# Second layers of a mixture of experts taken half by half, with longer runs of half-width output blocks, and logits transposed in the middle of the value products

## The chip, the cores and the metric

One core of a Trainium2 chip runs the whole kernel. The metric is the device time of one execution in microseconds (us), as the median of several executions. Lower is better.

## The reference

Causal attention with a per-step decay (8 batches, 8 heads, 576 positions, head size 64) is followed by a soft mixture of 8 experts. Cut to what matters here:

```python
scores = q @ k.T / 8 + cum[i] - cum[j]          # causal
x = softmax(scores) @ v                          # reshaped to 4608 rows x 512
logits = x @ phi                                 # 4608 x 32: 8 experts x 4 slots
d = softmax(logits, axis=0)                      # over the rows
slot_input = d.T @ x                             # 32 x 512
for e in range(8):                               # w1: 512 x 1024, w2: 1024 x 512
    slot_out[e] = relu(slot_input[e] @ w1[e]) @ w2[e]
c = softmax(logits, axis=1)                      # over the 32 slots
out = c @ slot_out                               # 4608 x 512, float32
```

All inputs and outputs are float32. The expert weights are 33.6 MB, the output is 9.4 MB.

## The kernel before, in words

**Attention.** The loop runs over 32 pairs of heads (`g`, four pairs to a batch). The order of all instructions is written out by hand, so each engine works through its queue in program order. For a pair, `s1` and `tops` find row maxima of the scores (TensorE, then VectorE), `s2` and `expo` make the exponentials (TensorE, then ScalarE), `causal` blanks the upper triangle (GpSimd), and `s3` multiplies them with the values: 50 small products in the order of the list `VALUES`, with 64 output partitions each, written to `pv`. `norm` divides by the row sums and writes `X`; `px` and `xcopy` transpose `X` for the logits.

**Logits of a batch.** One batch behind the attention, its logits are worked on amid the pairs; `w` counts the pairs from 0 to 3. At `w == 0` `logits` multiplies with phi. The result is 32 slots by 576 positions, folded into 128 partitions: columns 0 to 127 of the tile `LG` hold four blocks of 128 positions, and columns 128 to 191 of partitions 0 to 31 hold the last 64 positions. At `w == 1` `weigh` copies them to `LG`, `mgroup`, `mtop` and `mcast` find and spread the running maximum, `weigh2` makes the exponentials `EX`, `total` keeps the running sum `lrun`, and `tokens` transposes both `EX` and `LG` into one PSUM tile (`tk`), from which `LD` (the dispatch weights) is copied by ScalarE, and which `combine(b, 0)` reads on VectorE. `tk` takes its turn among three PSUM tiles (`ps_s`, tag `s`) with the score tiles of `s1`. The last 64 positions must come out in two partition halves, so they are doubled before the transpose: GpSimd copies them to the spare columns 192 to 255 of `EX`, and a second 128-wide transpose turns columns 128 to 255.

**Experts.** The weights come in quarters of 512 KB (`quarter`, 27 resident tiles and then buffers that have come free), all issued on SyncE's queue (`wload`, `wstream`) in the order that `STEPS` gives. `(e, 0)` is the first layer of expert e (four quarters, `mlp1`), `(e, 4)` and `(e, 6)` are two quarters each of its second layer (`mlp2`). For the experts below `DEFER` = 4 the quarters are cut by rows of w2 and give all 512 output columns at once; for the others (e, 4) gives columns 0 to 255 (half 0) and (e, 6) columns 256 to 511 (half 1). The results add up in PSUM in tiles of 32 partitions x 4.

**Output.** When half 0 of all experts is complete, `gathered`, `slots` and `halve` add up the four partition groups and spread the slot outputs to `SO`, in two float32r parts. `blocks` then multiplies the combine weights (`cT`, transposed by `cols`, two or three transposes at a step of `next(c[b])`) with `SO`, 128 rows of the output at a time; ScalarE and VectorE copy the results to a staging buffer in turn, and SyncE's queue sends it. Blocks with 256 columns (`half[0]`, `half[1]`) write 1 KB pieces to each output row, blocks with all 512 columns 2 KB pieces. The program before interleaves them with the half 1 products of experts 4 to 7 only:

```python
    mlp2(6, 1)
    blocks(2, 4, half[0])
    blocks(4, 6, half[0])
    mlp2(7, 1, 0)
```

13 of the 36 blocks go out in two halves, 23 whole.

Of the kernel before, what the change touches and what calls it, by code (L numbers as in the profile page):

```python
# [31 lines left out]
DEFER = 4  # L32

STEPS = tuple((e, 0) for e in range(8)) + tuple((e, k) for e in range(DEFER) for k in (4, 6)) + tuple((e, k) for k in (4, 6) for e in range(DEFER, 8))

SPLITS = {(6, 0): 4, (0, 6): 2, (1, 6): 3, (2, 6): 5, (3, 4): 6, (4, 4): 7}
# [39 lines left out]
def attn_softmoe(ctx: ExitStack, tc: tile.TileContext, qk, v, f, phi, w1, w2, cst, out):  # L76
# [314 lines left out]
    def weigh(b):  # L391
        if batch(b):
            plg = st["lg", b]
            if b < B - 1:
                nc.scalar.copy(LG[:, 0:128], plg[:, 0:128])
                nc.scalar.copy(LG[0:32, 128:192], plg[0:32, 128:192])
                nc.gpsimd.tensor_copy(EX[96:128, 192:256], LG[0:32, 128:192])  # L397
            else:
                nc.scalar.copy(LG[:, 0:192], plg[:, 0:192])
                nc.gpsimd.tensor_copy(EX[96:128, 192:256], LG[0:32, 128:192])  # L400
# [25 lines left out]
    def weigh2(b):  # L426
# [3 lines left out]
        if b < B - 1:  # L430
            nc.scalar.activation(EX[:, 0:192], LG[:, 0:192], AF.Exp, bias=mb[:, 1:2], accum_out=mb[:, 2:3])
            nc.gpsimd.tensor_copy(EX[0:32, 192:256], EX[0:32, 128:192])
        else:
            nc.scalar.activation(EX[:, 0:192], st["lg", b][:, 0:192], AF.Exp, bias=mb[:, 1:2])
            nc.vector.tensor_copy(EX[0:32, 192:256], EX[0:32, 128:192])
# [3 lines left out]
    def total(b):  # L439
# [5 lines left out]
        elif b < B - 1:  # L445
            nc.scalar.activation(lrun, lrun, AF.Identity, scale=mb[:, 3:4], bias=mb[:, 2:3])
# [3 lines left out]
    def tokens(b, *ns):  # L450
# [91 lines left out]
    nc.gpsimd.memset(EX[:, 192:256], 0.0)  # L542
# [182 lines left out]
    for g in range(1, NG):  # L725
# [19 lines left out]
        if w == 2:  # L745
            combine(b, 0)
# [98 lines left out]
        round_k(g + 3)  # L845
        if w == 1:
            weigh2(b)
            total(b)
        round_q(g + 3)
# [4 lines left out]
        if g == 31:  # L854
# [3 lines left out]
            split(1, 0)  # L858
        s3(g, VALUES[30:])
        if w == 0:  # L860
            logits(b, *range(NPAIR))
        if w == 1:
            tokens(b, 0, 1)
# [31 lines left out]
    next(c[0])  # L895
    tokens(b, 1)
    split(1, 1)
# [66 lines left out]
    def mlp2(e, half, *ks):  # L964

        for k in ks or range(2):
            w = weights(e, 4 + 2 * half + k)
            for n in range(4 if e >= DEFER else 2):
                if e < DEFER:
                    fc, to = 4 * half + 2 * k + n, pv[0]  # L970
                    start, stop = e == half == 0, e == DEFER - 1 and half == 1
                else:
                    fc, to = 4 * k + n, po[half][:, 0:256]
                    start, stop = e == DEFER and k == 0, e == NE - 1 and k == 1
                m = to.shape[1]
                step = m if start or stop else 256
                for c in range(0, m, step):
                    nc.tensor.matmul(  # L978
                        to[32 * (fc % 4) : 32 * (fc % 4) + 32, c : c + step],
                        HT[e][:, fc // 2, fc % 2, :],  # L980
                        w[:, m * n + c : m * n + c + step],
                        start=start,
                        stop=stop,
                    )
# [7 lines left out]
    for e, k in STEPS[:-4]:  # L992
# [26 lines left out]
        if (e, k) == (0, 6):  # L1019
# [4 lines left out]
        if (e, k) == (3, 6):  # L1024
            nc.scalar.copy(so, pv[0])
# [4 lines left out]
    stage = [t.rearrange("p a b -> p (a b)") for t in RAW] + p2 + p0  # L1030
    copies = [nc.scalar.copy, nc.vector.tensor_copy]

    def gathered(n):

        nc.vector.tensor_tensor(so[:, half[n]], so[:, half[n]], po[n][:, 0:256], op=ALU.add)
# [30 lines left out]
    mlp2(4, 1)  # L1066
    slots(0)
    mlp2(5, 1)
    halve(0)
    ring += [po[0], bank[0]]  # L1070
    blocks(0, 2, half[0])
    mlp2(6, 1)
    blocks(2, 4, half[0])
    blocks(4, 6, half[0])
    mlp2(7, 1, 0)
    blocks(6, 8, half[0])
# [61 lines left out]
```

## Time and profile before

| | |
|---|---|
| median of 3 runs | 390.42 us (388.98 to 390.79) |
| the profiled execution | 389.33 us, of which 387.6 us from its first to its last instruction |
| TensorE (PE) busy | 368.5 us, 95% of the span |
| VectorE (DVE), ScalarE (ACT), GpSimd (POOL) busy | 279.2, 274.3, 254.8 us |
| share of PE in the chain of work that ended last | 89% (DMA 3%, ACT 2%, DVE 2%) |
| DMA | 93.72 MB, mean 242 GB/s |

The chain of work that ended last is followed back from the last instruction to what released each step. PE stands for 89% of it. PEld is TensorE's weight load, SPq SyncE's queue. Matmuls are pipelined: the next one can start before the one ahead of it has ended, so a step between two starts says more than a duration. A float32 matmul leaves two records in the trace, a transpose or a float32r matmul one.

### The profile page before, as it was taken

How to read it: one execution, taken by the hardware profiler on the slowest of the kernel's cores; microseconds unless marked ns; L12 is line 12 of the kernel's file. 1: busy time of each engine (PE TensorE's matmuls, PEld its weight loads, DVE VectorE, ACT ScalarE, POOL GpSimd, SP SyncE). 2: the span in 40 equal slices, each digit the busy share in tenths (PEclk: the TensorE clock that was granted, in tenths of full speed). 3: DMA queues.
4: the chain of work that ended last, by engine and by line, in shares of the span. 5: the costliest groups of instructions: out<-in, count | busy, mean ns of one | idle time of the engine just before them, and what ended most of it. 6: DMA issues, size and time to landing. Idle time of an engine off the chain costs nothing.

```text
span 387.6 us, 15148 instructions
## 1 busy us (share of the span) xinstructions
PE 368.5 (95%) x5863; PEld 330.8 (85%) x5863; DVE 279.2 (72%) x1079; ACT 274.3 (71%) x670; POOL 254.8 (66%) x357
## 2 busy tenths in 40 slices
PE   8999999999999999999999999999999998999870
PEld 8889999999999999999999999999999985567640
DVE  7878787878887888788878887888787535441671
ACT  8969887878787878787878787878787553021560
POOL 4987887878787878787878787878787821000000
PEclk9999999999999999999999999999999999999995
DMA  6785878777777777777777777777777989996798
GB/s 206 199 203 153 241 223 269 201 226 201 231 210 218 214 214 215 215 216 213 214 215 217 212 215 215 215 216 214 212 224 208 280 316 361 416 418 258 269 391 317
DMA packets 34344, 93.72 MB, mean 242 GB/s; under 512 B 4266, under 2 KB 8288, under 8 KB 34272
## 3 DMA queue, kind: packets, MB, share of 16 engines
q1 hardware_dynamic: 34272, 92.75, 76.8%
q8 instruction: 46, 0.75, 0.8%
q14 instruction: 26, 0.21, 0.2%
HBM read 63.93 MB, written 9.73 MB: 190 GB/s over the span
## 4 chain that ended last, share of the span: by engine, by line
PE 89%; DMA 3%; ACT 2%; DVE 2%; issue 1%; POOL 1%; SPq 0%; ACTq 0%; POOLq 0%; DVEq 0%
PE pv L315 23%; PE ring L283 14%; PE s L230 13%; PE ring L284 12%; PE pv L342 4%; PE pv L978 4%; PE more L938 4%; PE lg L389 3%; PE ring L511 2%; PE ds L475 2%; DMA out<-RAW 2%; PE ring L1055 1%; DMA YA<-mr 1%; ACT PTS L290 1%; DMA WA<-cumd 1%
## 5 line engine op out<-in xcount | busy, mean ns | idle before, releaser
L290 ACT ACTIVATE PTS<-ring 128x320 f32<-128x320 f32 (+2 forms) x256 | 119.1, 501 | 39.1 <-PE ring L284 31.8
L283 PE MATMUL ring<-YA,WA 67*128 67x320 f32 (+9 forms) x384 | 119.0, 323 | 0.1
L246 DVE CUSTOM_DVE_ANT_0 s<-s,mask 128x320 f32<-128x320 f32 (+3 forms) x256 | 109.6, 446 | 5.6 <-PE s L230 0.9
L284 PE MATMUL ring<-YB,WB 128*128 128x320 f32 (+4 forms) x384 | 110.4, 296 | 0.0
L315 PE MATMUL pv<-V,PTS 128*64 128x65 f32 x3200 | 102.3, 223 | 0.1
L315 PEld LDWEIGHTS pv<-V,PTS 128*64 128x64 f32 x3200 | 97.2, 138 | 3.1 <-issue 1.6
L230 PE MATMUL s<-WA,YA 66*128 66x288 f32 (+9 forms) x384 | 97.9, 310 | 1.0 <-ACT YA L188 0.4
L209 POOL TENSOR_TENSOR WB<-RAW,WB 64x576 fp32r<-64x576 f32 x64 | 90.4, 1413 | 10.9 <-ACT WA L570 4.6
L214 POOL TENSOR_TENSOR YB<-RAW,YA 64x576 fp32r<-64x576 f32 x64 | 89.7, 1419 | 2.6 <-POOL EX L397 0.2
L283 PEld LDWEIGHTS ring<-YA,WA 67*128 67x128 f32 (+3 forms) x384 | 69.0, 181 | 5.8 <-issue 2.1
L284 PEld LDWEIGHTS ring<-YB,WB 128*128 128x128 f32 (+1 forms) x384 | 70.0, 182 | 0.0
L230 PEld LDWEIGHTS s<-WA,YA 66*128 66x128 f32 (+1 forms) x384 | 62.9, 190 | 6.8 <-ACT PTS L290 1.7
L301 POOL TENSOR_SCALAR_AFFINE_SELECT PTS<-PTS 128x128 f32<-128x128 f32 (+1 forms) x128 | 31.5, 268 | 21.9 <-ACT PTS L290 20.3
L246 DVE DVE_READ_ACCUMULATOR2_ANT MT<- 128x1 fp32r x310 | 44.0, 142 | 0.0
L183 ACT CAST WA<-RAW 64x576 fp32r<-64x576 f32 x64 | 40.2, 669 | 3.0 <-DMA RAW<-in_qk 2.1
L298 POOL TENSOR_SCALAR_AFFINE_SELECT PTS<-PTS 128x384 f32<-128x384 f32 x64 | 33.4, 523 | 12.2 <-ACT PTS L290 8.3
L188 ACT CAST YA<-RAW 64x576 fp32r<-64x576 f32 x64 | 40.3, 670 | 0.4
L246 DVE CUSTOM_DVE_ANT_0 s<-s,mask,MT 128x288 f32<-128x288 f32 x62 | 32.6, 526 | 10.0 <-PE s L230 1.4
L342 PE MATMUL pv<-cs,X 128*128 128x128 f32 x155 | 36.5, 272 | 0.0
L330 DVE TENSOR_SCALAR rl<-pv 128x5 f32<-128x5 f32 x64 | 10.5, 164 | 35.0 <-PE pv L315 24.7
L335 DVE TENSOR_TENSOR X<-pv,rl 128x320 f32<-128x320 f32 (+1 forms) x65 | 31.5, 486 | 2.4 <-DMA YA<-mr 0.3
L244 DVE TENSOR_REDUCE MT<-s 128x1 fp32r<-128x288 f32 x62 | 27.9, 450 | 0.0
(220 smaller groups left out, 386.5 us busy)
## 6 DMA issues: line engine op xcount, KB each, us to landing
w<-in_w SPq DMA_DIRECT2D x45, 512.0 KB
RAW<-in_qk SPq DMA_DIRECT2D x31, 576.0 KB
V<-in_v SPq DMA_DIRECT2D x32, 325.0 KB
YB<-YA SPq DMA_DIRECT2D x30, 288.0 KB
WB<-WA SPq DMA_DIRECT2D x30, 288.0 KB
p<-in_w SPq DMA_DIRECT2D x6, 512.0 KB
out<-RAW SPq DMA_DIRECT2D x6, 512.0 KB
out<-p SPq DMA_DIRECT2D x5, 512.0 KB
```

The costliest lines, as they stand in the source:

```text
L183: nc.scalar.copy(WA[g % 3][0:64, S * h : S * h + S], RAW[g % 3][64:128, h])
L188: nc.scalar.copy(YA[g % 3][0:64, h, 64:640], RAW[g % 3][0:64, h])
L209: nc.gpsimd.tensor_tensor(t[0:64], RAW[g % 3][64:128, h], t[64:128].bitcast(F32), op=ALU.subtract)
L214: nc.gpsimd.tensor_tensor(YB[g % 2][64:128, h], RAW[g % 3][0:64, h], YA[g % 3][0:64, h, 64:640].bitcast(F32), op=ALU.subtract)
L230: nc.tensor.matmul(t[:, o : o + w], ya[0:m, h, 128 * blk : 128 * blk + 128], wa[0:m, j0 : j0 + w], start=True, stop=True)
L246: nc.vector.tensor_tensor_reduce(out=t[:, o : o + w], in0=t[:, o : o + w], in1=mask[:, m0 : m0 + w], scale=1.0, scalar=top.bitcast(F32) if ...
L283: nc.tensor.matmul(o, wa[0:m, j0 : j0 + n], ya[0:m, h, 64 + i0 : 64 + i0 + w], start=True, stop=False)
L284: nc.tensor.matmul(o, wb[:, j0 : j0 + n], yb[:, h, i0 : i0 + w], start=False, stop=True)
L290: nc.scalar.activation(PT[i % 2][:, SEG_O[bank] : SEG_O[bank] + at], t[:, 0:at], AF.Exp, scale=0.125)
L298: nc.gpsimd.affine_select(d3, d3, pattern=[[0, 3], [1, 128]], compare_op=ALU.is_ge, fill=0.0, base=0, channel_multiplier=-1)
L315: nc.tensor.matmul(pvv[h][64 * u : 64 * u + 64, t, :], PT[h][:, at : at + 64], V[:, g % 2, c, 65 * h : 65 * h + 65], start=(c == 0), stop= ...
L342: nc.tensor.transpose(pm[:, 0:128], x[:, t, 128 * (p % 2) : 128 * (p % 2) + 128], ident)
```

## The change

It does five things.

- `STEPS` takes the second layers as half 0 of all eight experts, then half 1 of all. `DEFER` is gone, w2 is laid out by column halves for every expert, and both halves add up in one [128, 256] tile each.
- Blocks leave in half width in 12 runs of `early` (27 of 36 blocks, in groups of at most six between the half 1 products of experts 2 to 7); 9 blocks are left whole. Four more staging buffers are used. `cols` steps are spread differently.
- `tokens` transposes columns 0 to 127 as before, but turns the last 64 positions by two matmuls with a 32 x 32 identity, one for each partition half. The doubling copies of `EX` and `LG` go.
- At `w == 1` `tokens` and `combine(b, 0)` stand between the first 30 and the last 20 products of `s3`, instead of behind `s3` and in the next pair. Half of the rounding copies of ScalarE move behind them. The running sum moves from ScalarE to GpSimd.
- In the last batch `split(1, 1)` stands ahead of `tokens(b, 1)`.

```diff
-DEFER = 4
-STEPS = tuple((e, 0) for e in range(8)) + tuple((e, k) for e in range(DEFER) for k in (4, 6)) + ...
+STEPS = tuple((e, k) for k in (0, 4, 6) for e in range(8))
...
-            nc.gpsimd.tensor_copy(EX[0:32, 192:256], EX[0:32, 128:192])
...
-            nc.scalar.activation(lrun, lrun, AF.Identity, scale=mb[:, 3:4], bias=mb[:, 2:3])
+            nc.gpsimd.tensor_scalar(lrun, lrun, mb[:, 3:4], mb[:, 2:3], op0=ALU.mult, op1=ALU.add)
...
-        if 1 in ns:
-            nc.tensor.transpose(pm[:, 0:128], EX[:, 0:128], ident)
-        nc.tensor.transpose(pm[:, 128:256], EX[:, 128:256], ident)
-        if 0 in ns:
-            nc.tensor.transpose(pm[:, 256:384], LG[:, 0:128], ident)
+        for n in sorted(ns):
+            x, o = (LG, 256) if n == 0 else (EX, 0)
+            nc.tensor.transpose(pm[:, o : o + 128], x[:, 0:128], ident)
+            for u in range(2):
+                nc.tensor.matmul(pm[64 * u : 64 * u + 64, 224 - 96 * n : 256 - 96 * n], x[0:32, 128:192], ident[0:32, 0:32], start=True, stop=True)
...
+        if w == 1:
+            tokens(b, 0, 1)
+            combine(b, 0)
+            round_k(g + 3, 1)
+            round_q(g + 3)
         s3(g, VALUES[30:])
...
-        if w == 1:
-            tokens(b, 0, 1)
...
+    split(1, 1)
     tokens(b, 1)
-    split(1, 1)
...
     gathered(0)
-    mlp2(4, 1)
+    mlp2(0, 1)
     slots(0)
-    mlp2(5, 1)
     halve(0)
+    mlp2(1, 1)
+    more(5)
     ring += [po[0], bank[0]]
...
+    early = (((0, 2), (2, 4), (4, 6)), ((6, 8), (18, 20), (20, 22)), ((22, 24), (24, 27)), ((8, 10), (10, 12)), (), ((12, 15),), ((15, 18),))
+    turns = (5, 2, 2, 3, 3)
+    for e in range(2, NE):
+        for n in early[e - 2]:
+            blocks(*n, half[0])
+        mlp2(e, 1)
+        if e < NE - 1:
+            more(turns[e - 2])
     gathered(1)
...
+    for k, n in enumerate(n for run in early for n in run):
+        blocks(*n, half[1])
+        if k in (5, 8):
+            more(7)
+    for n in range(27, NT, 2):
+        blocks(n, min(n + 2, NT))
```

What this moves on TensorE at `w == 1`, before (`tk` is the tile of `tokens`, L315 the value products, L283 and L284 the next pair's scores):

```order
L315 MATMUL pv_150<-V,PTS 64x65 x21
L456 MATMUL tk_2643<-cs,EX 128x128
L457 MATMUL tk_2643<-cs,EX 128x128
L459 MATMUL tk_2643<-cs,LG 128x128
L283 MATMUL ring_152<-YA_93,WA_94 128x448
L284 MATMUL ring_152<-YB_91,WB_92 128x448
```

And in the changed program (line numbers are lower by one to five there):

```order
L314 MATMUL pv_150<-V,PTS 64x65
L452 MATMUL tk_2619<-cs,LG 128x128
L454 MATMUL tk_2619<-cs,LG 64x32 x2
L452 MATMUL tk_2619<-cs,EX 128x128
L454 MATMUL tk_2619<-cs,EX 64x32 x2
L314 MATMUL pv_150<-V,PTS 64x65 x20
L282 MATMUL ring_152<-YA_93,WA_94 128x448
L283 MATMUL ring_152<-YB_91,WB_92 128x448
```

Three transposes behind the values became two transposes and four matmuls of 64 output partitions ahead of the last 20 value products.

On TensorE at the end, before, from half 0 of the last expert on (L978 a quarter of a second layer, four matmuls; L1038 is `slots`, L1055 a block):

```order
L978 MATMUL pv_150<-w_121,w_136 32x256 x4
L978 MATMUL pv_149<-w_122,w_133 32x256 x4
L978 MATMUL pv_149<-w_123,w_133 32x256 x4
L1038 MATMUL more_5700<-ctok,cs 128x256
L978 MATMUL pv_149<-w_124,w_134 32x256 x4
L978 MATMUL pv_149<-w_125,w_134 32x256 x4
L1055 MATMUL ring_153<-SO,cT 128x256
L1055 MATMUL ring_151<-SO,cT 128x256
L978 MATMUL pv_149<-w_126,w_135 32x256 x4
L978 MATMUL pv_149<-w_127,w_135 32x256 x4
```

And in the changed program, from the same place (L966 a quarter, L1024 `slots`, L1041 a block, L705 the transposes of `cols`):

```order
L966 MATMUL pv_150<-w_113,w_136 32x256 x4
L966 MATMUL pv_149<-w_114,X_99 32x256 x4
L966 MATMUL pv_149<-w_115,X_99 32x256 x4
L1024 MATMUL more_5706<-ctok,cs 128x256
L966 MATMUL pv_149<-w_116,X_100 32x256 x4
L966 MATMUL pv_149<-w_117,X_100 32x256 x4
L705 MATMUL ring_153<-cs,w_136 128x128 x2
L1041 MATMUL ring_151<-SO,cT 128x256
L1041 MATMUL lg_5625<-SO,cT 128x256
L1041 MATMUL ring_152<-SO,cT 128x256
L1041 MATMUL ring_153<-SO,cT 128x256
L1041 MATMUL pv_150<-SO,cT 128x256
```

The first block stands eight quarters earlier in the work of the second layers; behind `slots` 14 quarters of half 1 are left instead of 6.

On VectorE in the last batch, before (L422 is the maximum, L435 the doubling copy, L464 `LD`, L696 `split(1, 1)`):

```order
L422 COPY mb_5730<-ring_153 128x1
L435 COPY EX<-EX 32x64
L464 COPY LD<-more_5700 128x160
L696 TENSOR_TENSOR cw_5671<-ctok,cw_5671 128x10x32
L900 TENSOR_REDUCE mb_5730<-EX 128x1
```

And changed:

```order
L419 COPY mb_5736<-ring_153 128x1
L690 TENSOR_TENSOR cw_5677<-ctok,cw_5677 128x10x32
L459 COPY LD<-more_5706 128x160
L897 TENSOR_REDUCE mb_5736<-EX 128x1
```

The doubling copy is gone, and the subtraction of `split` stands ahead of `LD` instead of behind it.

## Rows read from the trace of the kernel before

**Rows 1.** PE in order of time behind the value products: start, us, line, count

```profile
147.98 0.52 PE L315 MATMUL pv<-V,PTS 128*64 128x65 f32 x12
148.43 0.33 PE L456 MATMUL tk<-cs,EX 128*128 128x128 f32 x1
...
148.76 0.27 PE L459 MATMUL tk<-cs,LG 128*128 128x128 f32 x1
148.79 0.45 PE L283 MATMUL ring<-YA,WA 67*128 67x448 f32 x1
```

**Rows 2.** The page's group of value products: busy us, mean ns of one

```profile
L315 PE MATMUL pv<-V,PTS 128*64 128x65 f32 x3200 | 102.3, 223 | 0.1
```

**Rows 3.** PE between a transpose and narrow matmuls, in order of time

```profile
332.12 0.27 PE L459 MATMUL ring<-cs,LG 128*128 128x128 f32 x1
332.33 0.42 PE L938 MATMUL more<-w,EX 128*32 128x256 f32 x4
```

**Rows 4.** PE between a tiny matmul and another width, in order of time

```profile
320.61 0.21 PE L877 MATMUL more<-row,fin 1*1 1x32 f32 x2
320.75 0.32 PE L475 MATMUL more<-X,LD 128*32 128x128 f32 x4
```

**Rows 5.** PE in order of time, in the pair behind the tokens

```profile
150.15 0.38 PE L342 MATMUL pv<-cs,X 128*128 128x128 f32 x2
150.61 0.39 PE L230 MATMUL s<-WA,YA 97*128 97x320 f32 x1
```

**Rows 6.** DVE in order of time in the same stretch

```profile
150.15 0.32 DVE L496 TENSOR_TENSOR ctok<-tk,sm 128x160 f32<-128x160 f32 x1
```

**Rows 7.** Line L230's weight loads: what ended their idle time, us and times

```profile
  ACT PTS L290: 1.7, 6
```

**Rows 8.** ACT in order of time beside the value products

```profile
147.27 0.46 ACT L431 ACTIVATE EX<-LG,mb 128x192 f32<-128x192 f32 x1
...
149.47 0.28 ACT L464 COPY LD<-tk 128x160 f32<-128x160 f32 x1
```

**Rows 9.** DVE in order of time in the last batch

```profile
324.72 0.32 DVE L464 COPY LD<-more 128x160 f32<-128x160 f32 x1 [0.42 <-PE more L457]
324.96 0.48 DVE L696 TENSOR_TENSOR cw<-ctok,cw 128x320 fp32r<-128x320 f32 x1
```

**Rows 10.** PE in order of time in the last batch

```profile
325.86 1.30 PE L475 MATMUL pv<-X,LD 128*32 128x128 f32 x40
```

**Rows 11.** PE in order of time through the second layers and first blocks

```profile
344.29 1.29 PE L978 MATMUL pv<-p,X 128*32 128x512 f32 x10
...
351.21 4.57 PE L978 MATMUL pv<-w,w 128*32 128x256 f32 x80
...
357.78 1.07 PE L978 MATMUL pv<-w,w 128*32 128x256 f32 x16
358.78 0.39 PE L1055 MATMUL lg<-SO,cT 128*128 128x256 f32 x1
...
359.45 0.64 PE L978 MATMUL pv<-w,w 128*32 128x256 f32 x8
```

**Rows 12.** DVE in order of time: the ends of both `halve`

```profile
356.86 0.43 DVE L1042 TENSOR_TENSOR SO<-more,SO 64x256 fp32r<-64x256 f32 x1 [1.47 <-ACT SO L1041]
...
363.18 0.43 DVE L1042 TENSOR_TENSOR SO<-more,SO 64x256 fp32r<-64x256 f32 x1
```

**Rows 13.** The first output transfer on SyncE's queue

```profile
358.41 0.41 SPq L1058 DMA_DIRECT2D out<-RAW  x1
```

**Rows 14.** Stretches: us; busy us of PE, PEld, DVE, ACT, POOL; PEclk, DMA share, GB/s

```profile
356.50:359.00 2.50, 2.50 (x35) 1.20 (x28) 0.85 (x2) 0.69 (x2) 0.00 (x0) 1.00 0.00 0
...
361.00:363.50 2.50, 2.08 (x18) 1.34 (x10) 1.48 (x4) 1.38 (x5) 0.00 (x0) 1.00 1.08 380
...
365.50:370.00 4.50, 4.50 (x32) 3.94 (x32) 3.92 (x14) 3.90 (x11) 0.00 (x0) 1.00 1.01 333
370.00:385.50 15.50, 5.13 (x22) 2.95 (x20) 7.01 (x16) 5.23 (x10) 0.00 (x0) 0.81 1.05 400
```

More of the change, by code (lines that the diff above doesn't have):

```diff
@@ L31 @@
 QW = 1024
[L32 to L36 removed]
+STEPS = tuple((e, k) for k in (0, 4, 6) for e in range(8))
+SPLITS = {(6, 0): 4, (1, 4): 5, (2, 4): 2, (3, 4): 3, (4, 4): 6, (5, 4): 7}
 ORDER = [8 * e + k + n for e, k in STEPS for n in range(2 if k else 4)]
@@ L967, in mlp2 @@
             w = weights(e, 4 + 2 * half + k)
[L968 to L984, printed above, removed]
+            for n in range(4):
+                nc.tensor.matmul(
+                    po[half][32 * n : 32 * n + 32, 0:256],
+                    HT[e][:, 2 * k + n // 2, n % 2, :],
+                    w[:, 256 * n : 256 * n + 256],
+                    start=e == k == 0,
+                    stop=e == NE - 1 and k == 1,
+                )
     nc.vector.tensor_scalar_mul(mk, mk, fin[:, 2:3])
@@ L991, in attn_softmoe @@
     used = 0
-    for e, k in STEPS[:-4]:
+    for e, k in STEPS[:-8]:
         if k == 0:
@@ L1029, in attn_softmoe @@
     NT = B * S // P
-    stage = [t.rearrange("p a b -> p (a b)") for t in RAW] + p2 + p0
+    stage = [t.rearrange("p a b -> p (a b)") for t in RAW] + p2 + p0 + quarter[17:20] + quarter[26:27]
     copies = [nc.scalar.copy, nc.vector.tensor_copy]
     def gathered(n):
-        nc.vector.tensor_tensor(so[:, half[n]], so[:, half[n]], po[n][:, 0:256], op=ALU.add)
+        nc.vector.tensor_copy(so[:, half[n]], po[n][:, 0:256])
     def slots(n):
@@ L1065, in attn_softmoe @@
     gathered(0)
-    mlp2(4, 1)
+    mlp2(0, 1)
     slots(0)
-    mlp2(5, 1)
     halve(0)
+    mlp2(1, 1)
+    more(5)
     ring += [po[0], bank[0]]
[L1071 to L1076, printed above, removed]
-    blocks(8, 9, half[0])
-    blocks(18, 19, half[0])
-    mlp2(7, 1, 1)
+    early = (((0, 2), (2, 4), (4, 6)), ((6, 8), (18, 20), (20, 22)), ((22, 24), (24, 27)), ((8, 10), (10, 12)), (), ((12, 15),), ((15, 18),))
[6 more added lines that the diff above has]
+            more(turns[e - 2])
     gathered(1)
-    more(2, 1)
-    blocks(19, 20, half[0])
+    blocks(*early[-1][0], half[0])
     slots(1)
-    more(2, 1)
-    blocks(20, 21, half[0])
     halve(1)
-    blocks(21, 22, half[0])
-    more(2, 1)
+    more(6)
+    more(6)
     ring += [po[1], bank[1]]
-    then = {2: (2, 1), 4: (3, 2), 6: (3, 2), 18: (5, 2), 9: (5, 2), 13: (6, 2), 15: (6, 2), 22: (7, 2), 24: (7, 2)}
-    for n0, n1 in ((0, 2), (2, 4), (4, 6), (6, 8), (8, 9), (18, 20), (20, 22)):
-        blocks(n0, n1, half[1])
-        more(*then.get(n0, (B,)))
-    for n0, n1 in ((9, 11), (11, 13), (13, 15), (15, 17), (17, 18)) + tuple((n, n + 2) for n in range(22, NT, 2)):
-        blocks(n0, n1)
-        more(*then.get(n0, (B,)))
+    for k, n in enumerate(n for run in early for n in run):
[4 more added lines that the diff above has]
+        blocks(n, min(n + 2, NT))
 def kernel(q, k, v, f, moe_phi, moe_w1, moe_w2):
```

18 lines of the change are left out of this document (6 added, 12 removed).

## The prediction

> **What bounds the kernel now.** I read the chain of waits first: PE stands for 89% of it (the table above), in the attention and in the second layers alike. So a PE step that is added or removed there moves everything behind it. Next, the stretches at the end: DMA is idle from 356.5 to 359.0 and runs at 400 GB/s from 370.0 to 385.5 [rows 14]. The weights have landed by then and the last stage waits for output bytes. The reader is to see a kernel that is bound by PE until the second `halve`, and by output transfers behind it. The span is 387.6 us, the execution 389.33; its 1.73 us outside the span I leave alone. The median shown, 390.42, is 1.1 us above this execution: I sum against 389.33 and carry the difference over to the median.
>
> **Tokens amid the values (seven batches).** Before, the tokens stand on PE from 148.43 to 148.79: 0.36 us a batch [rows 1]. What replaces them has six matmuls of two widths, so the price hangs on what a change of width costs. The last value product begins at 147.98 + 0.52 - 0.22 = 148.28 [rows 1, 2], and the first 128-wide transpose 0.15 later, though value products follow each other every 0.03 (102.3 us / 3200) [rows 2]. A transpose that is followed by another 128-wide matmul costs 0.03 (148.76 to 148.79) [rows 1]; followed by a 32-wide one, 0.21 [rows 3]. A tiny 1 x 1 pair is followed by a 32-wide matmul 0.14 after its start [rows 4]. In all three, the next width begins 0.06 to 0.07 before the last matmul of the old width ends: PE runs nearly empty at each change. Before, there is one change of width between the values and the next pair's scores, 0.15, and the tokens stand behind it. Now there are five more starts of another width: values to transpose 0.15, transpose to 64-wide matmuls 0.21, those (two pairs of records, 0.02 longer than the tiny pair) to the next transpose 0.16, again 0.21, again 0.16 back to the values. Sum 0.89, less the 0.03 that the next value product would have taken: 0.86 against 0.36, so +0.50 a batch, +3.5 us for seven. Bounds: 0.33 instead of 0.27 for each transpose, as L456 has [rows 1], makes it +4.3; nothing paid at the narrow matmuls, 0.
>
> EX must be ready for its transpose. 40 records at 0.03 before 148.28 the thirtieth product begins, at 147.1, and the EX transpose 0.15 + 0.21 + 0.16 later, at 147.6. EX was ready at 147.27 + 0.46 = 147.73 [rows 8]; now one of the two rounding copies that stood ahead of it on ScalarE stands behind it, so it is ready sooner by that copy. No wait; if it came no sooner, 0.1 a batch.
>
> **The stall that goes.** In the next pair, the score matmul L230 begins at 150.61 though the transposes ahead of it were issued from 150.15 [rows 5]. It takes the PSUM tile that `tk` held, and `combine(b, 0)` reads that until 150.15 + 0.32 = 150.47 [rows 6]. The trace puts such waits down to ScalarE: 1.7 us in six [rows 7]. After the change `combine` follows the first `norm` about 1 us sooner, while PE comes 0.5 later: the wait goes, -1.7. What is late next is ScalarE, which now waits for the tokens before its `LD` copy and then has three rounding copies; before, it was not free until 149.47 + 0.28 = 149.75 either [rows 8]. I put its delay at 0.6 against PE's 0.5, and its exponentials have a ring of three PSUM tiles as cover: nothing. If that cover were gone, 0.1 a batch.
>
> The doubling copies (GpSimd), the memset and the running sum that moves to GpSimd are off the path: nothing waits for `lrun` until the last batch. Nothing gained, nothing lost.
>
> **The last batch.** PE begins the dispatch at 325.86 [rows 10], although `LD` was ready at 324.72 + 0.32 = 325.04: the transposes of `cols(1)` stand between, and wait for the subtraction of `split(1, 1)`, done at 324.96 + 0.48 = 325.44 [rows 9]. With the subtraction first, in time in which VectorE waits for ScalarE's exponentials, the dispatch can begin just behind `LD`, at 325.05: -0.8. The first layers follow on PE without a gap, so this reaches the second layers. Bounds: 0 and -0.8.
>
> **The end.** A quarter takes 8 records at (1.07 - 0.64) / 8 = 0.054, so 0.43 [rows 11]. Half 0 is complete behind 16 quarters instead of 24: 344.29 + 6.9 = 351.2 instead of 351.21 + 8 x 0.43 = 354.65 [rows 11]. From there to the first transfer it was 358.41 - 354.65 = 3.8 [rows 13]; now two transposes more, 0.2. First transfer: 355.2, 3.2 sooner.
>
> But PE then carries more before the second `halve`. From the first block (1.1 before its transfer, at 354.1): six pairs of quarters at 1.0 (357.78 to 358.78) make 6.0; 24 blocks in five runs, at 0.67 for a run of four (358.78 to 359.45), so 0.11 a block and 0.22 a run, make 3.7 [rows 11]; 13 transposes of combine weights at 0.12 (a third of the 0.36 of rows 1) make 1.5; waits for VectorE, which copies those weights between blocks, I put at 0.5 (0 to 0.8). That is 365.8, of which 0.3 is the step to another width. `gathered`, `slots` and `halve` took from 354.65 to 357.29, 2.64 [rows 12]: the second `halve` ends at 365.5 + 2.6 = 368.1, where it was 363.18 + 0.43 = 363.61 [rows 12]. It is 4.5 later.
>
> What is left to send behind it: 27 half blocks (3.54 MB) and 9 whole ones (2.36 MB) instead of 13 halves (1.70) and 23 whole (6.03). At 380 GB/s for 1 KB pieces (361.0 to 363.5) and 400 for 2 KB [rows 14]: 9.3 + 5.9 = 15.2 us instead of 4.5 + 15.1 = 19.6, so 4.4 less. It comes to 4.5 - 4.4 = +0.1. The 3.2 us that the first half wins are spent idle: data began about 0.7 behind the first issue (358.41, none before 359.0 [rows 13, 14]), so from 355.9 to the second half's data at 369.9 DMA has 14 us for 3.54 MB, or 9.3 us of work. I take +0.1, with bounds -0.4 (no waits for VectorE) and +1.4 (1 KB pieces at 333, as from 365.5 to 370.0 [rows 14]).
>
> **Sum.** 3.5 - 1.7 - 0.8 + 0.1 = +1.1: 390.4 for an execution like the profiled one, 391.5 as a median.
>
> **The rivals.**
>
> *Narrow matmuls without the drain* (faster). If the 64-wide matmuls share PE with the transposes, the tokens cost 0.36 as before, and the sum is -1.7 - 0.8 + 0.1 = -2.4: 388.0. Against it: rows 1, 3 and 4 have the same remainder of 0.07 at every change of width. 0.14.
>
> *The second half starts sooner* (faster). If blocks and transposes slip under the weight loads of the quarters, and the second `halve` ends near 364 instead of 368.1, the 4.7 idle us shrink by as much: -4.0, sum -2.9, 387.5. From 3.1 us sooner on it is faster by 0.5%. For it: PE's steps in the end are full of changes of width whose number I estimate; against it: each step's price is taken from the same stage. 0.15.
>
> *The stall stays* (slower). If `combine` or the `LD` copy ends later than 151.1, where PE then asks for the tile, the 1.7 is not won: 393.2. I have them done near 149.2. 0.12.
>
> *Small transfers run slower* (slower). At 333 GB/s for all 27 half blocks of the second half the end is 1.3 later: 392.8. For it: 333 was seen while half blocks went out; against it: 380 also was, with transfers of 256 KB. 0.14.
>
> The Trainium skill, "DMA: Bandwidth & Descriptors", section "Bandwidth", asks for at least 1 MiB a transfer to reach 75% of the peak, and lists 341 GB/s at 1 MB and 138 at 64 KB. By its 341 as a ceiling, the second half would take 10.4 us instead of 9.3, an estimate of 392.6. The 380 GB/s at 256 KB speaks against it, since several transfers are under way at once.
>
> **How the numbers follow.** The forecast and its own spread have 0.45 (390 to 392.3). About 0.5%, 2 us, is what a measurement of this kernel tells from no change. Faster than 388.5: the first two rivals for the most part and little else, 0.25. Slower than 392.4: the last two and the upper bound of the tokens, 0.30. Same: 0.45. The range, 387.6 to 393.7, reaches to the first rival and past the last two.
>
> **What would show it.** Right: from the thirtieth value product to the next one some 0.9 us at `w == 1`; L230 without its wait; a dispatch 0.3 us behind the tokens in the last batch; first output transfer about 3 us sooner against the last quarter of the first layers, and a second `halve` about 4.5 later; DMA idle in two or three places between. Wrong: narrow matmuls within 0.1 us of the transposes, no idle DMA before the second half, or the end of the second `halve` far from 368 plus what came before it.

## The result, and the profile after

The changed kernel takes 393.02 us (median of 6 runs, 392.72 to 393.4), the kernel before 389.44 on the same chip (6 runs, 388.59 to 390.79): a ratio of 1.0089, interval 1.0066 to 1.0112. The forecast was 391.5, range 387.6 to 393.7. The sign is right and the time is inside the range, but +1.1 us was forecast and +3.6 came. The profiled executions, 389.33 and 393.35, differ by 4.0, and their spans, 387.6 and 391.6, by 4.0 too. That is the sum taken apart below.

The page of the changed kernel, engines first: busy time, share of the span, instructions.

```profile
PE 374.0 (96%) x5948; PEld 333.4 (85%) x5948; DVE 280.0 (71%) x1085; ACT 273.4 (70%) x670; POOL 253.9 (65%) x347
```

PE is still the engine to look at, so I followed it through the three places of the change. PE amid the values of the same batch as [rows 1]: start, us, line, tile, count.

```profile
147.68 0.46 PE L314 MATMUL pv<-V,PTS 128*64 128x65 f32 x10
148.07 0.33 PE L452 MATMUL tk<-cs,LG 128*128 128x128 f32 x1
148.33 0.30 PE L454 MATMUL tk<-cs,LG 32*64 32x32 f32 x4
148.56 0.33 PE L452 MATMUL tk<-cs,EX 128*128 128x128 f32 x1
148.82 0.30 PE L454 MATMUL tk<-cs,EX 32*64 32x32 f32 x4
149.06 0.34 PE L314 MATMUL pv<-V,PTS 128*64 128x65 f32 x4
```

The last product before the tokens begins at 147.68 + 0.46 - 0.22 = 147.92, the next one behind them at 149.06. That is 1.14 us, where I had put 0.89. Each next width begins 0.07 before the last matmul of the old one ends, as in [rows 1, 3, 4]: 148.07 + 0.33 - 0.07 = 148.33, 148.33 + 0.30 - 0.07 = 148.56. So the rule held at these five steps, and the durations put into it were too short. (It does not hold at every change of width, as the experiments show.)

Line L229 (L230 before): its matmuls, then what its weight loads waited for, in us and times, as in [rows 7].

```profile
L229 PE MATMUL s<-WA,YA x384: 191/298/471, 8.4 to 308.5; 66*128 66x320 f32 x42, 66*128 66x288 f32 x42, 66*128 66x448 f32 x42, 97*128 97x320 f32 x22
...
  ACT YA L187: 1.2, 2
  DVE LG L245: 0.2, 1
```

The entry of 1.7 us in six [rows 7] is gone: the stall went as forecast. In the last batch, PE in order of time:

```profile
328.10 0.44 PE L705 MATMUL more<-cs,cw 128*128 128x128 f32 x2
328.59 0.64 PE L470 MATMUL pv<-X,LD 128*32 128x128 f32 x16
```

and DVE there:

```profile
327.01 0.48 DVE L690 TENSOR_TENSOR cw<-ctok,cw 128x320 fp32r<-128x320 f32 x1
328.21 0.33 DVE L459 COPY LD<-more 128x160 f32<-128x160 f32 x1 [0.72 <-PE more L454]
```

The subtraction is out of the way and the dispatch begins right behind `LD`: 10.14 us behind the first value product of the last pair, where it was 10.88. At the end, both `halve` on DVE:

```profile
356.20 0.43 DVE L1028 TENSOR_TENSOR SO<-more,SO 64x256 fp32r<-64x256 f32 x1 [1.44 <-ACT SO L1027]
...
371.22 0.43 DVE L1028 TENSOR_TENSOR SO<-more,SO 64x256 fp32r<-64x256 f32 x1 [0.72 <-ACT SO L1027]
```

the first transfer on SyncE's queue:

```profile
357.92 0.41 SPq L1044 DMA_DIRECT2D out<-RAW  x1
```

and the stretches from the second `halve` on (columns as in [rows 14]):

```profile
368.00:370.00 2.00, 2.00 (x24) 1.16 (x22) 1.68 (x6) 0.49 (x2) 0.00 (x0) 1.00 0.00 0
370.00:372.00 2.00, 1.62 (x10) 1.21 (x10) 1.20 (x5) 1.18 (x4) 0.00 (x0) 1.00 0.81 285
372.00:374.00 2.00, 2.00 (x17) 1.93 (x15) 2.00 (x8) 1.75 (x7) 0.00 (x0) 1.00 0.56 188
374.00:376.00 2.00, 2.00 (x16) 1.81 (x14) 2.00 (x8) 1.85 (x7) 0.00 (x0) 1.00 0.65 225
376.00:378.00 2.00, 1.86 (x9) 1.56 (x9) 2.00 (x8) 1.70 (x5) 0.00 (x0) 1.00 1.09 382
```

Counted from the first second-layer product (347.15), the first transfer leaves at 10.8, where it was 14.1, and the second `halve` ends at 24.5, where it was 19.3. DMA stands still before it, as forecast. What was not forecast: it still runs at 225 GB/s from 374 to 376, when the second half has long been there.

For each kernel below I took four distances from its profiled execution, in us: from the first value product of the pair that holds the third batch's tokens to that of the next pair; from the first value product of the last pair to the first second-layer product; from there to the end of the second `halve`; and from there (the first second-layer product again) to the end of the span.

```
kernel           tokens' pair  last pair to   second   end    median   ratio to before, interval
                               second layers  halve
before              10.62         29.31        19.32   43.34
after               11.06         28.70        24.50   44.48  393.02   1.0089  1.0066-1.0112
a_old_tokens        10.62         28.57        24.50   43.26  387.74   0.9979  0.9965-0.9992
b_tokens_alone      11.06         29.46        19.31   43.29  392.97   1.0118  1.0099-1.0137
e_split_first       10.60         28.57        19.31   43.25  387.97   0.9980  0.9970-0.9990
i_combine_early     11.53         30.64        19.32   43.28  395.76   1.0177  1.0155-1.0199
f_both_small        11.51         28.58        19.31   43.27  394.39   1.0133  1.0112-1.0154
c_one_width         10.60         28.63        24.51   43.24  388.85   0.9991  0.9979-1.0004
d_grouped           10.80         28.70        24.50   44.31  391.23   1.0051  1.0031-1.0071
h_less_second       11.06         28.70        22.01   40.78  389.46   1.0009  0.9997-1.0021
k_more_warm         11.06         28.71        24.51   43.25  409.92   1.0518  1.0495-1.0542
k2_old_more_warm    10.62         28.57        24.52   43.24  411.94   1.0577  1.0552-1.0601
j_act_copy          11.74         28.57        24.50   43.23  394.03   1.0145  1.0103-1.0186
l_three_runs        10.62         28.58        23.71   42.43  387.36   0.9954  0.9937-0.9972
```

Where two kernels have the same code, the first and third columns repeat to 0.02 us, the others to 0.1, but for the 30.64 that is explained below. The kernels ran in several sessions, each with runs of the kernel before beside them: its median was 388.71 beside those from a to i, 390.14 beside k, k2 and j, 388.81 beside l, so kernels of different sessions are compared by their ratios. One slow run of j_act_copy (399.79) is left out; the other five lie between 393.53 and 398.11, and the profiled one is the slowest of them. Ahead of the fifth pair, executions differ by up to 0.8 us by chance (57.9 to 58.7, without the two kernels that change the start); the kernel before was at 58.63 in the execution shown, the changed one at 58.22.

### The profile page after: what moved, and what is told of

It is laid out like the page before. It is cut to its first block, busy times and chain, and to the rows that moved or that the text cites. A ratio compares the mean times of both kernels' runs of the same rounds, so it can differ in the third digit from the quotient of the medians.

```text
span 391.6 us, 15316 instructions
## 1 busy us (share of the span) xinstructions
PE 374.0 (96%) x5948; PEld 333.4 (85%) x5948; DVE 280.0 (71%) x1085; ACT 273.4 (70%) x670; POOL 253.9 (65%) x347
## 4 chain that ended last, share of the span: by engine, by line
PE 94%; DVE 2%; issue 0%; ACT 0%; DVEq 0%; ACTq 0%
PE pv L314 26%; PE ring L282 15%; PE s L229 13%; PE ring L283 13%; PE pv L341 4%; PE pv L966 4%; PE more L935 4%; PE lg L388 3%; PE ring L506 3%; PE ds L470 2%; PE tk L452 1%; PE ring L1041 1%; PE tk L454 1%; PE ring L705 1%; PE pv L255 1%; PE more L1041 1%
## 5 line engine op out<-in xcount | busy, mean ns | idle before, releaser
L282 PE MATMUL ring<-YA,WA 67*128 67x320 f32 (+9 forms) x384 | 119.3, 324 | 0.0
L283 PE MATMUL ring<-YB,WB 128*128 128x320 f32 (+4 forms) x384 | 110.5, 296 | 0.0
L314 PE MATMUL pv<-V,PTS 128*64 128x65 f32 x3200 | 103.6, 223 | 0.0
L229 PE MATMUL s<-WA,YA 66*128 66x288 f32 (+9 forms) x384 | 97.9, 311 | 0.4 <-ACT YA L187 0.4
L213 POOL TENSOR_TENSOR YB<-RAW,YA 64x576 fp32r<-64x576 f32 x64 | 89.6, 1417 | 2.5
L282 PEld LDWEIGHTS ring<-YA,WA 67*128 67x128 f32 (+3 forms) x384 | 69.0, 181 | 6.3 <-issue 2.1
L283 PEld LDWEIGHTS ring<-YB,WB 128*128 128x128 f32 (+1 forms) x384 | 69.9, 182 | 0.0
L229 PEld LDWEIGHTS s<-WA,YA 66*128 66x128 f32 (+1 forms) x384 | 63.0, 190 | 5.5 <-ACT YA L187 0.8
```

The lines of the kernel that those rows point to most:

```text
L213: nc.gpsimd.tensor_tensor(YB[g % 2][64:128, h], RAW[g % 3][0:64, h], YA[g % 3][0:64, h, 64:640].bitcast(F32), op=ALU.subtract)
L229: nc.tensor.matmul(t[:, o : o + w], ya[0:m, h, 128 * blk : 128 * blk + 128], wa[0:m, j0 : j0 + w], start=True, stop=True)
L282: nc.tensor.matmul(o, wa[0:m, j0 : j0 + n], ya[0:m, h, 64 + i0 : 64 + i0 + w], start=True, stop=False)
L283: nc.tensor.matmul(o, wb[:, j0 : j0 + n], yb[:, h, i0 : i0 + w], start=False, stop=True)
L314: nc.tensor.matmul(pvv[h][64 * u : 64 * u + 64, t, :], PT[h][:, at : at + 64], V[:, g % 2, c, 65 * h : 65 * h + 65], start=(c == 0), stop= ...
```

## The experiments

**The three parts apart.** First the attention undone, then each of two parts alone.

```diff
# a_old_tokens: after, with the attention's part of the change reversed
-        if w == 1:
-            tokens(b, 0, 1)
-            combine(b, 0)
-            round_k(g + 3, 1)
-            round_q(g + 3)
         s3(g, VALUES[30:])
...
+        if w == 1:
+            tokens(b, 0, 1)
```

> The changed kernel with the attention of before: doubling copies, tokens behind the values, combine in the next pair, running sum on ScalarE. The last batch's order and the end stay changed. Theory (the tokens amid the values cost about 0.45 us a batch net, the end about +1, the last batch -0.75): the seven batches give back 3.1 to 3.5 us, so 389.5 to 390, level with the kernel before within 0.5 us. Rival (the half blocks at the end cost most of the 3.6): it stays above 392.

The reverse is the kernel before with the lines on `weigh`, `weigh2`, `total`, `tokens` and the loop over pairs as they stand in the change's diff:

> The kernel before with the changed attention alone (tokens amid the values, narrow matmuls, combine early, running sum on GpSimd), its own last batch and end. Theory: +0.45 us a batch net, so +3.1 to +3.5 (392.5 to 393), with the wait of the next pair's scores for the tile gone. Rival (the attention is even and the end costs): within 1 us of before.

```diff
# e_split_first: before, with one line moved
+    split(1, 1)
     tokens(b, 1)
-    split(1, 1)
```

> The kernel before with one line moved: the subtraction of split(1, 1) ahead of the last batch's tokens. Theory: the dispatch begins 0.75 us sooner and all behind it moves along, -0.75. Rival (the first layers wait for weights, or the end for its transfers, and hide it): 0.

The attention alone costs 4.3 us (392.97 against 388.71), the reordered subtraction wins 0.74 (387.97), and with both of the other parts in place but the old attention the time is 387.74: the new end adds nothing, 43.26 against 43.25 to 43.34. The attention carries the loss, as the theory had it, and a little more than its 3.1 to 3.5. The old-tokens kernel lies below its 389.5 to 390, since I had charged the end with 1; and the kernel before took 388.71 in that session, 0.7 less than beside the changed one.

**Is it the width or the place?** In the same place, the tokens first in the width of the value products, then with fewer changes of width.

```diff
# c_one_width
-            nc.tensor.transpose(pm[:, o : o + 128], x[:, 0:128], ident)
+            for u in range(2):
+                nc.tensor.matmul(pm[64 * u : 64 * u + 64, o : o + 128], x[:, 64 * u : 64 * u + 64], ident, ...)
             for u in range(2):
-                nc.tensor.matmul(pm[64 * u : 64 * u + 64, ...], x[0:32, 128:192], ident[0:32, 0:32], ...)
+                nc.tensor.matmul(pm[64 * u : 64 * u + 64, ...], x[:, 128:192], ident[:, 0:32], ...)
```

> The changed kernel with its tokens in the width of the value products: each transpose as two matmuls of 64 columns of weights against the identity, the narrow ones with all 128 rows and 64 columns, so that no width changes amid the values. Theory (the price is paid at the changes of width, 0.15 to 0.26 us each): the insertion falls from 1.14 us to 0.5 to 0.65 (two pairs of 128-column matmuls at an estimated 0.2, from four times the 0.07 of a pair of 32 columns less its start, and two of 0.07), -0.5 to -0.6 a batch, -3.5 to -4.2 for seven: 389 to 389.5. Rival (the place costs: ScalarE's copies and roundings come late behind it): within 1 us of the changed kernel, 392 to 393.

> The changed kernel with the same six token matmuls in another order: both transposes, then the four narrow ones. Three changes of width in place of five. Theory: 0.15 + 0.11 + 0.20 to 0.26 + 0.22 + 0.15 = 0.83 to 0.89 in place of 1.14, so -0.25 to -0.31 a batch, -1.8 to -2.2: 390.8 to 391.2. Rival (the place costs, not the widths): no change, 393.

PE in order of time, the kernel in one width:

```profile
146.89 0.81 PE L314 MATMUL pv<-V,PTS 128*64 128x65 f32 x22
147.53 0.39 PE L453 MATMUL tk<-cs,LG 128*64 128x128 f32 x4
147.75 0.26 PE L455 MATMUL tk<-cs,LG 128*64 128x32 f32 x4
147.84 0.42 PE L453 MATMUL tk<-cs,EX 128*64 128x128 f32 x4
148.09 0.26 PE L455 MATMUL tk<-cs,EX 128*64 128x32 f32 x4
148.17 0.43 PE L314 MATMUL pv<-V,PTS 128*64 128x65 f32 x8
```

and the grouped one:

```profile
146.21 1.34 PE L314 MATMUL pv<-V,PTS 128*64 128x65 f32 x40
147.48 0.33 PE L452 MATMUL tk<-cs,LG 128*128 128x128 f32 x1
147.65 0.27 PE L452 MATMUL tk<-cs,EX 128*128 128x128 f32 x1
147.85 0.30 PE L456 MATMUL tk<-cs,LG 32*64 32x32 f32 x4
147.99 0.28 PE L456 MATMUL tk<-cs,EX 32*64 32x32 f32 x4
148.20 0.27 PE L314 MATMUL pv<-V,PTS 128*64 128x65 f32 x1
```

In one width there are more matmuls, and from the last product before them (146.89 + 0.81 - 0.22 = 147.48) to the next it is 0.69 in place of 1.14; grouped, 148.20 - (146.21 + 1.34 - 0.22) = 0.87. The pair of the tokens follows to 0.02: 10.60, 10.80 and 11.06. The rounding copies, the running sum and `combine` stand in the same place in all three, so it is the changes of shape that cost. The Trainium skill, "TensorEngine Tiling (Array Packing)", says under "Key Properties" that a change of the tiling mode drains TensorE; these rows agree, and give the price: 0.15 behind a value product or a narrow matmul, 0.26 behind a transpose that has another shape ahead of it, against 0.03 from one value product to the next.

"Width" is not the right word for what changes. The narrow matmuls have 32 rows and 64 columns of weights and the value products 128 and 64 (32\*64 and 128\*64 in the rows), so the step back to the values (0.15) has no change of width, but one of rows. And a change of width alone need not cost anything: in the changed kernel's score products, 64 columns are followed by 128 after 0.06, 0.16 before the first one's end.

```profile
316.30 0.22 PE L283 MATMUL ring<-YB,WB 128*64 128x64 f32 x1
316.36 0.45 PE L282 MATMUL ring<-YA,WA 67*128 67x448 f32 x1
```

A value product has the same 128\*64 and is followed by the same L282 after 0.15, in all 24 places where the two meet. One difference is that the value products write either half of the output partitions and these score products the first 64 alone; no run tests whether that decides. The one-width kernel took over the rows, the columns and the halves of its neighbours together.

Even in one width the move wins nothing. Against the old-tokens kernel its pairs of tokens are level in the five batches with a stall (0.70 - 0.36 is paid, 0.33 won) and 0.29 and 0.22 longer in the first and the seventh, which have none.

The grouped kernel came out at 391.23, just above its forecast of 390.8 to 391.2, the one-width kernel at 388.85, under its 389 to 389.5. What the one-width kernel has beyond its forecast is the end: 43.24, where the changed kernel has 44.48.

**What the stall hangs on.** Attempts to win it without moving the tokens.

```diff
# i_combine_early: before, with
-        if w == 2:
-            combine(b, 0)
...
         if w == 1:
             tokens(b, 0, 1)
+            combine(b, 0)
```

> The kernel before with combine(b, 0) moved from the next pair to right behind the tokens, nothing else. Theory: the 0.33 us that the next pair's scores wait for the tile of the tokens goes in five or six batches, -1.7 at no price, since the tokens stay behind the values at 0.36 us. Rival (VectorE is held up by waiting for the tokens and its own later work comes late): 0 or up to +1.

> The kernel before with two small moves: split(1, 1) first in the last batch, and combine(b, 0) right behind the tokens. Theory: -0.75 and up to -1.7 add up, 387 to 388.7; better than both kernels. Rival: the two hide each other or the end absorbs them, within 0.5 us of before.

Both are misses by a wide margin: +7.1 and +5.7 us. The stall itself is gone in both: the score matmul L230 follows the transposes after 0.03 in every batch, where before it was 0.35 to 0.38 in five. So it did hang on the read of `combine`; the price comes up elsewhere. DVE in order of time, of the kernel with `combine` early:

```profile
151.26 0.33 DVE L495 TENSOR_REDUCE sm<-tk 128x5 f32<-128x160 f32 x1 [1.44 <-ACT LD L464]
151.62 0.33 DVE L496 TENSOR_TENSOR ctok<-tk,sm 128x160 f32<-128x160 f32 x1
151.86 0.15 DVE L330 TENSOR_SCALAR rl<-pv 128x5 f32<-128x5 f32 x1
```

and its waits, the line of PE that waited longest (us, times, longest):

```profile
PE pv L342 <- DVE X L335: 6.6, 7, 1.1
```

`combine` now stands on DVE ahead of the second head's `norm` (L330 to L335). It waits 1.44 us, in the end for ScalarE's `LD` copy, and all of that time `norm` waits behind it; the transposes of X (L342) then wait on PE, up to 1.1 us in each of seven batches. The rival named the mechanism, but I had given it at most +1. In the changed kernel `combine` has the whole rest of the values as cover: DVE's L491 runs from 149.86 to 150.18, and the second `norm` begins at 150.49. In the kernel with `combine` early alone the last batch is 1.3 us longer too (30.64). The granted clock accounts for it: 0.50, the lower of the two levels, from 331.47 to 334.88, right behind a wait of 0.81 us for the subtraction of `split(1, 1)`; the 40 records of the dispatch take 2.36 us there instead of 1.30 [rows 10].

```profile
331.47:334.88 3.41, 3.41 (x45) 2.52 (x46) 0.89 (x4) 0.37 (x1) 0.54 (x2) 0.50 1.00 401
```

With the subtraction first that wait is gone, and that kernel's execution has no such fall there (28.58). The same wait in the kernel before is not followed by one.

```diff
# j_act_copy: a_old_tokens, with
             copy(LD, pm[:, 0:160]...)
+        if 0 in ns and b < B - 1:
+            nc.scalar.copy(ctok[:, b], pm[:, 224:384]...)
...
-            lt = st["tok", b][:, 224:384]...
+            lt = ce if b < B - 1 else st["tok", b][:, 224:384]...
```

> The old-tokens kernel with one copy more on ScalarE a batch, that of the turned logits from the tile of the tokens to SBUF, right behind the LD copy; combine reads the copy. Theory (the next pair's scores wait 0.33 us for combine to have read the tile): the tile is free 0.5 us sooner, the wait goes in five or six batches, and ScalarE's 0.28 us more lie ahead of exponentials that have a ring of three tiles as cover: -1.7, some 386. Rival (ScalarE's copy delays the exponentials and so the products): 0 to +2.

A miss again, 394.03, and not by the rival's way. (The stall is gone here too: 0.03 in every batch.) DVE of that kernel, in order of time:

```profile
150.53 0.32 DVE L496 TENSOR_REDUCE sm<-ctok 128x5 f32<-128x160 f32 x1 [0.45 <-ACT ctok L465]
150.88 1.27 DVE L497 TENSOR_TENSOR ctok<-ctok,sm 128x160 f32<-128x160 f32 x1
152.07 0.45 DVE L243 TENSOR_REDUCE MT<-s 128x1 fp32r<-128x288 f32 x1
```

GpSimd beside it:

```profile
149.16 2.81 POOL L213 TENSOR_TENSOR YB<-RAW,YA 64x576 fp32r<-64x576 f32 x2
```

and the line L497 over the whole run (ns least, median, most; first and last start):

```profile
L497 DVE TENSOR_TENSOR ctok<-ctok,sm x7: 324/1270/1285, 72.9 to 313.1; 128x160 f32<-128x160 f32 x7
```

With the logits in SBUF the same subtraction of 128 x 160 takes 1.27 us in place of 0.32 [rows 6], and ends 0.2 behind GpSimd's L213 (149.16 + 2.81 = 151.97). `MT` comes 1.1 later, counted from the pair's first value product, and PE waits for it. The Trainium skill, "SBUF — State Buffer", section "Who interferes with whom", says that a tensor-by-tensor operation of VectorE with both inputs in SBUF contends with GpSimd's reads; these rows agree. Which of the two goes first decides: in the first and the seventh batch the subtraction began 0.04 and 0.06 before GpSimd's operation and took 0.33 and 0.32, and GpSimd's took 1.57 and 1.55 instead of 1.42. So in five batches the attempt traded 0.33 us of stall for a longer one, the pair of the tokens is 1.1 longer (11.74 to 10.62), and ScalarE's cover was not tested. The profiled execution also has 3.4 and 6.8 us at a granted clock of 0.50, from 234.40 and 275.36 on, both soon behind such a wait:

```profile
276.00:278.00 2.00, 2.00 (x24) 1.84 (x26) 1.80 (x9) 0.85 (x3) 0.52 (x1) 0.50 0.06 11
```

Three pairs are 1.2 to 1.9 longer there than the like pairs before them, 4.6 in all, which is what this execution (398.11) has over the fastest (393.53).

**The end.** Does the kernel wait for the second half?

```diff
# h_less_second: after, with
-                    stop=e == NE - 1 and k == 1,
+                    stop=(e == (4 if half else NE - 1)) and k == 1,
...
-        mlp2(e, 1)
+        if e < 5:
+            mlp2(e, 1)
```

> The changed kernel without the half 1 products of experts 5, 6 and 7 (left out of the sum, so half the output columns lack them); all blocks, weights and transfers stay. Six quarters less between the blocks, some 3 us of PE. Theory (the end waits for the second halve while DMA runs dry; each us that it comes sooner ends the kernel as much sooner, until DMA is never idle): -2.5 to -3. Rival (the end is set by the bytes that leave in 1 KB pieces from the first transfer on): 0 to -0.8.

The second `halve` comes 24.50 - 22.01 = 2.49 us sooner, and the end 43.26 - 40.78 = 2.48 against the old-tokens kernel, which has the same end. The theory stands: with DMA dry, each us of the second half is a us of the kernel. Against the changed kernel itself the end is 3.7 sooner, 1.2 more than the second half explains.

**The 1.2 us.** The changed kernel and the grouped one have an end of 44.48 and 44.31, all others with the same end 43.23 to 43.26, though the second `halve` and the copies of the blocks fall in the same place. SyncE's queue at that issue, in the changed kernel:

```profile
373.68 1.55 SPq L1044 DMA_DIRECT2D out<-w  x1
```

and in the old-tokens kernel:

```profile
369.23 0.45 SPq L1046 DMA_DIRECT2D out<-w  x1
```

and DMA's queues of the changed kernel from 373.4 to 374.9 (packets, MB, share):

```profile
q1 hardware_dynamic: 465, 0.46, 87.4%
q8 instruction: 1, 0.02, 5.6%
```

Both issues are 26.53 behind the first second-layer product. In the changed kernel the queue stands 1.1 us longer in that one issue, and no other can leave. From 373.4 to 374.9 its DMA rows have a packet of instructions; the other kernel's same stretch (368.9 to 370.4) has none. The grouped kernel has two such issues, 1.35 us at 371.78 and 2.18 at 357.09, and a packet of instructions beside each.

```diff
# k_more_warm: after, with
-    warm(WARM[0], fy)
+    warm(3, fy)
+    warm(48, fy, 32)
# k2_old_more_warm: a_old_tokens, with
-    warm(WARM[0], fy)
+    warm(66, fy, 32)
```

> The changed kernel with 40 more, shorter warm-up matmuls ahead of everything (3 of 192 columns and 48 of 32 in place of 11 of 192; their results are not used). In the changed kernel one issue of an output transfer takes 1.55 us on SyncE, in the grouped one 1.35, where the one-width and the old-tokens kernels take 0.45, and the last stage is 1.1 to 1.2 us longer in the first two. Just those two show a 16 KB load of instructions at that moment. Theory (the loads come every so many PE instructions, and the one that meets that issue delays it): with 40 more matmuls ahead the load falls elsewhere, the issue takes 0.45, the stretch from the first second-layer matmul to the end falls from 44.5 to 43.3, and the time by 1.1, to 392 or less. Rival (chance, or another cause): the stretch stays at 44.5.

> The reverse: the old-tokens kernel with 55 more warm-up matmuls (66 of 32 columns in place of 11 of 192), which gives it as many PE instructions ahead of its end as the changed kernel has. Theory: the load of instructions now meets the issue behind the second half's first blocks, that issue takes 1.4 to 1.6 us, and the stretch from the first second-layer matmul to the end grows from 43.3 to 44.4; some 388.8 in place of 387.7. Rival: it stays at 43.3.

The first confirms the forecast for the end: 43.25. The issue that took 1.55 takes 0.46, on SyncE's queue:

```profile
390.89 0.46 SPq L1045 DMA_DIRECT2D out<-w  x1
```

and the stretch that ran at 225 GB/s, as far behind the first second-layer product, is full:

```profile
391.20:393.20 2.00, 2.00 (x16) 1.81 (x14) 2.00 (x8) 1.84 (x8) 0.00 (x0) 1.00 1.09 382
```

Its total is no use, since the short warm-ups cost 17 us at the start, which I had not expected: PE was still slow behind them (the score matmul of 97x288 takes 0.69 at 26.19, where in the changed kernel it takes 0.43 at 8.98). The reverse failed: the loads of instructions did not fall on that issue, so its 43.24 says nothing either way.

What is shown is that the delay goes when the number of PE instructions ahead of it changes, and that the three long issues coincide with a load of instructions. In all traces together eleven output issues began while a load of 16 KB ran. Six of them took 0.63 to 2.18 us, and each of the six ended 0.39 to 0.41 behind the load's end, as if it had begun only there. The other five took 0.37 to 0.44, two of them begun well inside a load (359.82 in the kernel before, 355.11 in the one-width kernel). So a load can hold an issue and need not; that it is the load which holds it is inferred, and what decides stays open.

**A better end.** Fewer changes between blocks and products, with the old attention.

```diff
# l_three_runs: a_old_tokens, with
-    for e in range(2, NE):
-        for n in early[e - 2]:
-            blocks(*n, half[0])
-        mlp2(e, 1)
-        if e < NE - 1:
-            more(turns[e - 2])
+    plan = ((early[0], (5, 2)), (early[1] + early[2], (2, 3, 3)), (early[3] + early[4] + early[5], ()))
+    for e, (runs, turns) in zip((2, 4, 6), plan):
+        for n in runs:
+            blocks(*n, half[0])
+        mlp2(e, 1)
+        mlp2(e + 1, 1)
+        for n in turns:
+            more(n)
```

> The old-tokens kernel with the first half's blocks and the second half's products in three long turns instead of six short ones: blocks of two turns together, then the half 1 products of two experts, then the transposes. No instruction more or less, three changes between blocks and products fewer. Theory (each such change costs PE 0.3 to 0.5 us, and each us that the second halve comes sooner ends the kernel as much sooner): second halve 1.0 to 1.5 us sooner against the first second-layer matmul (24.5), and so the end (43.3), 386.3 to 386.8. Rival (longer runs of blocks wait for the two engines that copy them): no gain, or up to 1 us lost.

The second `halve` ends 0.79 sooner (23.71), the end 0.83 sooner (42.43): somewhat under the 1.0 to 1.5, and again us for us. The time, 387.36, is above the forecast 386.3 to 386.8 accordingly. PE in order of time, where two experts' products now follow each other without a step:

```profile
358.06 1.93 PE L968 MATMUL pv<-w,w 128*32 128x256 f32 x32
...
362.38 1.93 PE L968 MATMUL pv<-w,w 128*32 128x256 f32 x32
```

At 0.9954 of the kernel before (0.9937 to 0.9972) it has the lowest ratio here, and is faster than both kernels; its interval still meets that of the old-tokens kernel (0.9965 to 0.9992), and what it has over that one is the end in the trace.

## Why the prediction was right and where it was off

The spans differ by 4.0: -0.4 ahead of the fifth pair (chance), +3.9 from there to the last pair, -0.6 from there to the second layers, +1.1 at the end.

- **Tokens amid the values: the term that was mis-sized.** Forecast +0.50 a batch, 3.5 in all; the pairs give 0.44 to 0.46 in each of five batches whose stall went (0.33), 0.79 in the first, which had none (10.27 to 11.06), and 0.63 in the seventh, which had none either: 3.7 (the other 0.2 lies in pairs without tokens, 0.13 of it in one), so 5.3 without the stall. The mechanism was right at these five steps, but not "at every change of width", as the score products show. The sizes: "transpose to 64-wide matmuls 0.21" was read from a transpose that is the last of a run (0.27 long); one that has another shape ahead of it runs 0.33, so the step is 0.26, which I had as an upper bound only. And "those (two pairs of records, 0.02 longer than the tiny pair) to the next transpose 0.16": the last of the four narrow records begins 0.08 to 0.09 behind the first and 0.15 before the next transpose, so 0.23. Twice 0.05 and twice 0.07 make the 0.25 that was missing. One reading did not enter the sum: a transpose followed by another transpose costs 0.17 (148.43 to 148.76 for two, rows 1), not the 0.03 that holds behind the last one.
- **The stall that goes:** -1.7 forecast, -1.7 found (0.33 in five batches); no other wait took its place in the changed kernel.
- **The last batch:** -0.8 forecast, -0.74 alone. In the changed kernel 0.13 of it is lost again with the new tokens of that batch (28.70 against 28.57).
- **The end:** +0.1 forecast. Without the delayed issue it is -0.1 to 0 (43.24 to 43.26 against 43.25 to 43.34). Two errors cancelled in it: the second `halve` is 5.2 later, not 4.5, and what follows it is 5.3 shorter (24.02 to 18.76), not 4.4. That the term came out near is luck. The +1.1 on top is the issue, a wait that no row of before showed.
- **The rivals.** The narrow matmuls are paid for like the transposes (0.26, 0.15). The second half does not start sooner. The stall does not stay. Half blocks are sent at 382 GB/s [rows 14 had 380 and 333], so small transfers are not the reason; the low rate from 374 to 376 goes with the long issue (382 in the kernel with more warm-ups).

So the stall and the last batch held, the end held by two errors that cancelled, but for an event outside the sum, and the price of the tokens was 1.8 us too low. The time lies inside the range because the range reached to 393.7, not because the sum was near: 1.8 and 1.1 us were missing from it.

## What to carry to other kernels

Where rows show that a change of shape costs, an insertion of small matmuls is to be priced by its changes, each at the full duration of the last matmul before it less what overlaps; read that duration from a matmul with the same kind of neighbour ahead of it. Give small matmuls the rows, columns and output partitions of their neighbours, even if that takes more of them. Compare the price with the wait that is to be won: here 0.33 was to be won in five batches of seven. Before an operation that waits is moved up on an in-order engine, look at what stands behind it there, and who waits for that.

## What the runs showed of the hardware

- Where a change of shape cost PE time, the cost followed from the matmul before it, not from the one behind: 0.15 behind value products and narrow matmuls (0.22 long), 0.26 behind a transpose with another shape ahead of it (0.33 long). A change of rows alone (32\*64 to 128\*64) cost the same 0.15, and one from 64 to 128 columns among the score products took 0.06.
- A VectorE subtraction took 0.32 us with one operand in PSUM, and 1.27 with both in SBUF where an operation of GpSimd (L213) had begun before it; where it began first itself it took 0.32, and GpSimd's operation 0.13 to 0.15 more.
- An output issue on SyncE took 1.35 to 2.18 us in place of about 0.45 in three cases, each beside a load of instructions and ending 0.4 behind it; others beside such a load took 0.4. Among the last transfers of every kernel issues take 0.7 to 1.2 also where there is none.
- At the start, warm-up matmuls of 32 columns took two thirds of the time of those of 192, and PE was still slow behind 22.6 us of them. The kernel with 40 more shows 102 records in 22.61 us, of which 96 are of 32 columns; with 6.81 / 22 = 0.31 for each of the other six that is 0.22 a record. PE in order of time:

```profile
1.88 22.61 PE L506 MATMUL ring<-WB 128*128 128x192 f32 x102 [1.88 <-DVE ring L525]
```
